# A Conformer block on one core: a ring of 12 query chunks, 15 probability tiles, the first input chunk in two DMAs, and a plan derived anew

## The chip, the cores and the metric

The kernel runs on one core of a Trainium2 chip. The core has five engines that work side by side and wait for each other through semaphores: TensorE (PE in the profile, with PEld for its weight loads), VectorE (DVE), ScalarE (ACT), GpSimd (POOL) and SyncE (SP, which here only issues DMAs). TensorE writes its results to PSUM, which this kernel uses as eight banks of 512 float32 columns; the other tensors live in SBUF, 128 partitions wide. The metric is the device time of one execution in microseconds (us). Lower is better.

## The reference

The input `x` has 2 sequences of 4000 tokens with 144 features, in bfloat16. The reference is one Conformer block:

```python
h = layernorm(x);  x = x + 0.5 * (silu(h @ w_ff1a) @ w_ff1b)         # 144 -> 576 -> 144
h = layernorm(x);  q, k, v = split(h @ w_qkv)                        # 4 heads of 36
p = softmax(q @ k.T * 36 ** -0.5);  x = x + (p @ v) @ w_o            # 4000 x 4000 per head and sequence
h = layernorm(x);  a, b = split(h @ w_pw1);  h = a * sigmoid(b)
c = sum over i of pad(h)[i : i + T] * dw[i]                          # 5 taps along the tokens
x = x + silu(c) @ w_pw2
h = layernorm(x);  x = x + 0.5 * (silu(h @ w_ff2a) @ w_ff2b)
return layernorm(x)
```

The attention is by far the largest part: 2 x 4 x 4000 x 4000 exponentials, 128 million of them.

## The kernel before

**Chunks.** The 8000 tokens are cut into 16 chunks of 500 (`NCH` = 16, `CH` = 500), eight for each sequence (`CPB` = 8). A chunk is stored as 4 blocks of 125 tokens. Everything except the attention works on one chunk at a time: `pre(c)` makes the first feed-forward and the projections to queries, keys and values; `post1(c)` takes the attention's result through `w_o` and the gated linear unit; `post2(c)` makes the convolution, the second feed-forward, the last layernorm and the store.

**Attention.** For a chunk of queries the kernel goes through the keys of its sequence in 62 tiles of 64 keys and a last one of 32. The scores of one tile for all four heads are four matmuls of 64x64 weights and 500 columns (`scores`, L1731), each in its own quarter of the PE array, into a pair of PSUM banks. The exponential of a tile is taken in one of two ways:

- On ACT (`emit_exp`, L1758): one ACTIVATE with Exp over 1000 columns, from the pair of banks into one slot of `PT`. There are 806 of these, and 16 of 500 columns for the last tiles.
- On DVE (`dve_tile`, L1772): two TENSOR_SCALAR of 500 columns that turn the scores into 16-bit integers whose bits are an approximate power of two, then two bit operations and one product over 1000 columns, with the result split over two slots of `PT`. There are 186 of these tiles.

The probabilities are then multiplied with the values (`o_quads`, L1808): four matmuls for each used slot of `PT` (eight for a DVE tile, as it leaves two slots), which add up over all tiles of the chunk in the last two PSUM banks (`BX` = 6). A column of ones in the values gives the sum of the softmax. So a DVE tile takes one exponential off ACT, and costs five DVE instructions and four matmuls more on PE.

**Buffers that the change touches.** `PT` has `NPT` = 11 slots (L592). `QT` (L754) holds the projected queries of all 16 chunks, 2 x 8000 columns of bfloat16. It also serves as scratch memory: when a chunk c is finished, `epilogue(c)` (L1668) copies the two PSUM banks as float32 over the queries of chunks c-1 and c (`OTF`, L1670), which are no longer needed, and transposes them from there. The first two chunks are processed in two halves (`phases`, L1718: first the keys of the first five chunks, then the others, since the later keys come late); the sums of the first half wait in `SAVE` (L1658), which lies over the queries of later chunks. `proj` (L1258) computes queries and keys; a condition keeps a projection from being issued while its place still holds `SAVE`.

**What sets the order.** At build time a planner runs through the whole kernel with its own costs for every operation. Each chunk's work is a generator that asks for an engine, a bank or a slot (`need`), and `pick_any` (L1912) chooses what comes next. Its choices are steered by `POLICY` (L603), 20 tables of 49 values, one for each stretch of 21 key tiles; `due` (L2005) decides by them whether a tile goes to DVE. The planner records the operations. After that, `reorder` (L283) moves blocks of operations on each engine by the offsets written in `ORDER` (L38), one character for a block, and `PLACES` (L115) assigns the PSUM banks. `R.cut()` begins a new block. In the end every engine has a fixed list of instructions; it runs this list in order and waits at an instruction whose inputs, slot or bank are not ready. All instructions are emitted by one helper, so the profile puts nearly all of them on L402 and they are told apart by tile names.

**Start and end.** At the start SP loads `X` chunk by chunk (L841 for chunk 0), while ACT issues the loads of the first weights. In the end, when no attention is left, the planner switches to a mode ("tail") in which SiLU is taken by ACT directly; for this a dummy activation on `DUM` (L2063) loads the other function table. Before that, SiLU is made of a Tanh on ACT (tile `TH`) and a product on DVE (tile `HT`, `SW`).

Of the kernel before, what the change touches and what calls it, by code (L numbers as in the profile page):

```python
# [21 lines left out]
TB = 125  # L22
# [12 lines left out]
FILLS = (5, 2, 5, 12, 3, 1, 3, 0, 0, 0, 0, 0, 0, 0)  # L35
# [16 lines left out]
        "MPPPPWOPPQOXJPPVOJOOYQNIOOOOPNPPPSOSOPQQUQOGPZPPPPQHPPaOJOOOXNQQMMVZMMMEMNUNPNLOPTOOROMSOZNTPLRRMMIO"
        "]OOOOQOMOOOOQYMOOOOQOMOQOPPPPPPSOOOPPTPNPNPPPPQQNPPPPPPPPYYVPRLJP]]HPITOPNQJMOSgOSSORKTLQNd2RKMMRLNS"
        "SLMQQRJSNRY]LOPPM:SOMKPQLPQQNRROMRRRMVLQNNXO_LNNNNNNPPRLNNZQQSPTINOHSPLRRMaTLPPLLRTTLLLMSLNVVOWOMORW"
        "ENSVVN[MJNRMOVVOMOMOSQORROR^RNRROR)JNRNNNRROQRRJNRRRNWSJNOMOQNYOOOPSMNXMMOSNNOMZSNNNPMOPWMNVNNNNNOdP"
        "NOOQQMQLNOOOOORPNLPPPPQOZOPPPSSPIVVQQNVOQUUOQN??RSOZOKOOOROOLQNPPPRO^QMNQQMWOKNOMNRRORVINQQMMQQNWTQM"
        "NLNSPSQKWQOURPW[QUQQTRX>DRR@QEQQQQQaPPPPPPPR=QRLLQOLXXNNNOOLNRRRRMYSOZNDOLOYNOXNNGNNNNOgQNROOPUOPNXQ"
        "QLBKNOMNPNSSOOLZRNNSPPMUUOGPWJPPJUOQQ^QKHOOPNRRMTROJJQOPPPZOOSNNNPZOOJOOOOOPNROOPPPPPQOPPPPQTQMNOPPP"
        "TOOOSNPVMUNNOMNRRNNQORR[NLOZNNNNNNRTLL_LP`LNPQLXPJORINIOQUHOQVMMPNOOPTOQNNPQRROUPTOOOQQQTTWPMMYOO:NO"
        "OOOQZPPPPPPZPNORTNP?USPIKNP_OOOOOOOOOSOPNKQOPPPQRP[LOOOOOPQOPKYOOOOQNNOZNQNNOOOPPRLOPPPPPQOPPQOPPPPP"  # L60
        "PPPPPPTOPNOWWOQWNOIWWOGRIOMVP[GQYNQWJRLFSSKRTIPEQTMPNORORNOPROQNQOQQVPUKNNNNXbNNNNNNNNOQNNOROOQQQQHP"
        "bOOQNNOOOOSZNNPJLRPMKQRMQSPLOPPRROTROJRROVJOOPSSNUU]OOSTTObEQQLFYQQM`LNNNNNYP/LNNNNNNPPROOSQXNLOOQNN"
        "OPROOPP]OOOQQNLSN]^LMKNNOMPMOQKRRXQUHPPIOK_OOOOOOOOOOOQNNPQYNOOQRM]RKRSQISQWJFOROIiMOPROOK^XXMMMMNNX"
        "MSPGMI^>MOPQQLQQNJPQRRKXPPTJNNNNPQQNPPPZOPNYPMMOMNNOOPPPPPQQRPSQOI]O[NNNYMOOQNNQHUZDOOOPPQQG_LPPMOOP"
        "NOQNNZNNOOOXNNNO[LNNNOOOOOOWNOWOMYMMMQMMVOMNOOOQTNOOOPROOPPVOOYNOOLOOOOQTXLNOQOPJOXOOOOQOMOWSPURKKLU"
        "LOXPNLOOOPQMQQNQRNOUQNPMQQQQKSQUSQSVMWPGETYOKSJPNSYRNFKQWMMOMQUMRLNRROTQINUUQNSJLMRRTMVRcMTHNRSNSFNO"
        "ZFOOLPMRVKSLLOWLPPMQUMVVKMMPLMWTQMMMUMQUUMNINRRLNPPPRRSZMOJPPMPeMNNUPMOOORROQSEZIPMXJMNNNSULQKLSNPNP"
        "ZOOSNNOMOPNPPPPPPPPPPPRRTQVKQNPRGSPPKSOORNOPPPPQOPPPPPPPQQQSSPRRRGWRSQTTTKBHYRJRNQKYOOJTNNNNRMQNQQTM"
        "OZNNYOMWMOOOJOIPTO[RNLMOWRNLROTWZOGGMNOWOKNPTTQNLWPVPDPNUNQHNO[QRSLLORKQNLPPSOOOUQRMOQQQQRPFPPPPROOP"
        "TQNPMQTPQORPQSQOEQORRTVPLQQHTKOOOPQOPROOPPPPPPVOPPMOOPQQNPUOQQMRRKNSXOOLQNPMOPPQOPQOWQNRMNSQRMJPTPNP"  # L70
        "NPPPPTTNOVVRRNJMTPTUVNORJNSSOO8YOOOOPRMNNPPUURNNKTQKUUQMJMUQQQRRHJPSSNNaM`NNPPLLPSYPJJVNNPPSSSSSSL??"
        "PPPPTTTOOSQIIggPNLNQQMSLNVMMQQRRR@TTGGDQMROOPPSOOOQSSPLMQQN"
    ),
    "act": (
        "PPPPPPPPPPPPPPSOOOSQNNPQOPPQOPQOPWOOOOOOOPPPQRRTLMSUSLLSLMOPPPPPPPPPPPPQOPPQOPPPPPPPPQOPPPPPPPPPPPPP"
        "PPPQOPPPPPPPPPPPPPPPPPPPPPPPPPPPPPPPPPPPPPPPPPPPPPPPPPPPPPPPPPPPPPPPPPROOROQNPQOPPPPPPPPPPPPPPPPPQOP"
        "QQNPPQOPPPPPPPPPPPPPPPPPPPPPPPPPPQOQOQOPPPPPPPPPPPPROOPPPPPPPPPPPPPPPPPPQOPPPPPPPPPPPPPPPPPPPQOPPPPP"
        "PQOQOPPPPPPPPQOPPPPPPPPPPPPPPPPPPPPPPQOPPPPPPPPPPPPPPPPPROQNPQQNPPPPPPPPPPPPPQOPPPPPPPPQOPPPPPPPPPPP"
        "PPPPPPPPPPPPPPPPPSOOOPPPPPPPPPPPPPPPPPPPPPPPPPPPPPPQQNPPPPQOPPPPQQNPPQOPPQOPQOQOPPPPQOQOPPPPPPPPPPPP"
        "PPPPPPPPPPQOPPPPPPPPPPPPPPPPPPPPPPPPPPQOPPROOPPPPPQOPPPPPPPPPPQOPPPPPPPPPPPPPPPPPPPPPPPPPPPPPQOPPPPP"  # L80
        "QOQOPPQOPPPQOPPPPPPPPPPPPPPPPPPPPPPPPPPPPPPPQQNPPPPPQOPPPPPPPPPPPPPPPPPPPPPPPPPPPPPPPPPPPPPPPPPPPPPP"
        "PPPPPPPPPPPPPPPPPPPPPQOPPPPPPPPPQOPPPPPPPPQOQOQOPPPPPPPPPPPPPPPPPPPPPPPQOPPPPPPPPPPPQQQMPPPPPPPPPPPQ"
        "OQOQOPPPPPPPPPPPPPPPPPPPPPPPQOPPPPPPPPPPPPPPPPPPPPPPPPPPPPPPPPQOPPPPPPPPPPQOPPPPPPPPPPPPPPPQOPPPQOPP"
        "PPPPPPPPPPPQOPPPPPPQOPPPPPPPPPPPPPPPPPPPPPPPPPPPPQOPQOPPPPPPQOPPPPPPPPPPPPPPPPPPPPPPPPPPPPPPPPPPPQOP"
        "PPPPPPPPPPPPPPPPPQOPPPPPPQOQOPPPPPPPQOPQOQTNPNOPROQNQQQMPPPPROOSQNNPQSNOSSSLMMPPPPPPPPPQQNPPROO"
    ),
    "dve": (
        "PQRPQQQJPROQaMOOOQRaMNJNOPLRNNYYHOOKNPIRNQJQQNRROQQQQIWSPPR_OaPGGOQQKQKTWSNSTEGWRSENFNVQRLMXMNORNNPM"
        "QQNPQOPQOPPPROOPPPPQOPPPPPPPPPQOQOPPRPRSQRRTQQRRSTPSSTRURUQRURRSTRSWSQRVSUVQSUU$US2T!DSQoTQOPSQOS@SC"
        "MRLRPQyRHNQGLOLNNOMNOPNOOOPNPNPQMPRORNOPrOOPQRLRLR=OLPNOPNOPNOOOOOOOWOMOMOPLQRRMSPLOPPSPPQQQVPPPPPDP"  # L90
        "PPQOPPQOROOQOQOROOQOPcPNOOOOPQOQKNOOOOPNQOQQTMVNNPMOOPPPPQQVPSPJRRKRSQSTPUUWNSF@LLOPPPPPUPUPPQRIQQRP"
        "QRWQNQOPP=QOPPPROOPUPNOPNPPPPQQ_PLOOQNPPLO]NOOLOOPNOOSQMQLSOROQRRRNRGVNQOQOKPPPPPPPPPPTOTOOLOPPRPQSS"
        "OSSPLRPDRPNPPPPPQOPQOQRROQQQQHROQQQQQVQOGOTOMPQQSQRNQQRROSSASNRXQRPRTOSSSS@RJRSOR=QRPRSOHSPRSQJQRPTP"
        "SOOXRBNNPNOSNOSNOSNPNPROOSOOOPQOQOTPNOOVOOQNPMPPPVPNPPMOPROOZQNPQOPQOPGPPPPQOPPPPPPQOPPPPQOPPPPPQQTP"
        "URUQTKPEQQGROOUQOQOQTPTOORDNQOQOPQQNRSOTLNOOSOOOQOQSPTQKPTPJROSPRRNQQTPTRNRSQSQTHP9O`PPQOPPPPPPEOOPN"
        "PRPNQOQOQOPPPPPPQOPPPPPPROOTOOOORRNSMPNPROOPPPPPRfNNOPNPNOOOOOOPQMNOOSNNOPPPPPPPPPQOROOPPPPRRNRPQKPP"
        "PPUOOOROMQRNORPNPQOQQNSOOOPQOQRNQRMQNQQNPPPPPROOPPPPPQOTPPPRKOPQOQOPPVPPVOOOPPSQENSOOOPPPPPSQORPRPRP"
        "RPUDOQORPQQTPPPQDPQOPPPROOPROOQQNQOPPQOPPPPPPQOPPPPPPPPPPPPPPPPQOPPTYPTLSPJKLOPPQOPPRORNOROOPPPPPPPP"
        "PPQQQQQKQRNOPPPQOPPQOPPTPPMOROOQOQOSOOSNOOPPPPPUOOOOOPVOPPPLpNOOOPWOLNNNNNNOPNOOOOQNQMQMQOLOQQRMRNOP"
        "PPPPPPPPPPPPPPQOQOROOROQNPPPPPQOPPROOPPPPPPPPPPPPQOPPPPQOPPPPPPPPPPPPPPROOPROQQMPPPPQQNRTNSMRMRLOPPQ"  # L100
        "OPQOXPRPRPJRRIQLPPPQOPQOPPQOPQOPSPNRPRPRPQHPSOORNOPQOQORPNUROMNQNUPNTNOPLRROMQOPSSNRMMPPQOPPPPPPSOOO"
        "PPPROOQOPPPPPPPXPQOPPSOOQFQOPPPPPPQOQOSOSOTQSMINPPPQRNOQOUOOORORLTNPSMPVPKPNPRMOQOPQOQQNRPRPLPPPRSNP"
        "RPKPQOQOPPQOPPROOSOOOPROOQOQQQQQRPTPPSOSOBOPPPROSNPSPPSTRSMRRKCRPQMPROQNPQOPPPPPRTOMPQRLOQOQQQSQSeMO"
        "PQOPScUNNOPSPGQQSST4EHSNROSPSEV[]OQ_RSFGOHSGINKQNQRSKPYPQJNOQNNO"
    ),
    "pool": (
        "PQQQQRSOPRPQTQOPQQSPROQQQQQRROQQQQQQQ,PXOOOOOOOXNOQNTM[NLMSNNOPLPNQTQMSMPWPQOPHWTMQLMPSPUOHQOQUKPPPQ"
        "QJPQQQMPPQOQOSOOSNOQNPPRPNQQN"
    ),
    "sp": (  # L110
# [448 lines left out]
def bass_standalone__conformer_family_zipformer__speech_kernel(  # L559
# [1108 lines left out]
    def epilogue(c, part):  # L1668
# [27 lines left out]
        for zz in range(2):  # L1696
            bk = yield need("pe", banks, dur=0.44)
            for i in range(NB):
                if i == 2:
                    R.cut()  # L1700
# [406 lines left out]
```

## Time and profile before

| what | us |
|---|---|
| median of 3 runs (883.4 to 884.31) | 883.54 |
| the profiled execution, its whole time | 883.61 |
| its span, first to last instruction | 881.5 |
| PE busy, instructions | 852.0, 11403 |
| ACT busy, instructions | 850.7, 1096 |
| DVE busy, instructions | 815.1, 1799 |
| POOL busy, instructions | 300.0, 584 |

The share that a busy time has of the span is an average over three parts: the first 20 us, in which the attention has not started; the attention until about 846 us; and 35 us behind it, in which the last chunks are finished. Two instructions that follow each other on ACT or DVE overlap in the records: the next one starts before the one in front has ended. So the duration that a group row gives (1084 ns for the large exponential) is longer than the time by which the engine's queue moves on, which is read from starts in the timeline. The granted clock of TensorE is 0.998 of the full one.

### The profile page before, as it was taken

The page shows a single profiled execution, that of the slowest core. Times are in us where ns is not written, and L with a number is a line of the kernel's source. Part 1 is how long each engine was busy: PE and PEld are TensorE (multiplying, and loading weights), DVE is VectorE, ACT ScalarE, POOL GpSimd, SP SyncE. Part 2 cuts the span into 40 slices and gives each one's busy share as a digit, 9 for nine tenths or more (in the row PEclk, how much of TensorE's full clock was granted, in tenths as well). Part 3 has the DMA queues.
Part 4 walks back from the last instruction along what each step waited for, and adds up shares of the span by engine and source line. Part 5 has one row for each costly group of instructions (what it writes and reads, how often), then busy time and mean ns, then how long its engine had stood idle before and what let it go on. Part 6 is the DMA issues. An engine that isn't in the chain of part 4 may idle for free.

```text
span 881.5 us, 26988 instructions
## 1 busy us (share of the span) xinstructions
PE 852.0 (97%) x11403; PEld 378.4 (43%) x11403; DVE 815.1 (92%) x1799; ACT 850.7 (97%) x1096; POOL 300.0 (34%) x584
## 2 busy tenths in 40 slices
PE   8999999999999999999999999999999999999996
PEld 6544333444344434334344344443433343444465
DVE  7978999999999999989988899997988999999997
ACT  6799999999999999999999999999999999999984
POOL 7761600215235324125203432045351036031434
PEclk9999999999999999999999999999999999999999
DMA  3231010201211210211101111002011001101101
GB/s 100 44 66 36 22 37 2 63 22 39 51 30 23 51 24 14 52 24 39 28 17 30 30 29 31 23 16 51 22 37 23 15 9 37 24 22 37 30 23 33
DMA packets 114221, 28.80 MB, mean 33 GB/s; under 512 B 101085, under 2 KB 114100, under 8 KB 114100
## 3 DMA queue, kind: packets, MB, share of 16 engines
q1 hardware_dynamic: 112642, 26.46, 13.7%
q8 instruction: 89, 1.46, 0.7%
q10 hardware_dynamic: 1458, 0.62, 0.3%
q14 instruction: 32, 0.26, 0.1%
HBM read 13.44 MB, written 13.61 MB: 31 GB/s over the span
## 4 chain that ended last, share of the span: by engine, by line
ACT 45%; PE 33%; DVE 19%; DMA 1%; issue 1%; SPq 1%; ACTq 0%; DVEq 0%
ACT PT L402 40%; PE PS L402 33%; DVE PT L402 11%; ACT TH L402 4%; DVE HT L402 2%; DVE ST L402 1%; DVE X L402 1%; DVE XN L402 1%; DVE QT L402 1%; SPq L402 1%; DVE KT L402 1%; DMA X<-in_x_dram 1%; DVE AN L402 0%; DMA XTQ<-rows 0%; DMA WE<-in_w_ff1a_dram 0%
## 5 line engine op out<-in xcount | busy, mean ns | idle before, releaser
L402 ACT ACTIVATE PT<-PS 128x1000 bf16<-128x1000 f32 (+1 forms) x822 | 758.2, 1075 | 1.7 <-PE PS L402 0.6
L402 PE MATMUL PS<-QT,KT 64*64 64x500 bf16 x3968 | 424.6, 385 | 13.1 <-ACT PT L402 7.5
L402 PE MATMUL PS<-PT,VA 64*37 64x500 bf16 x4712 | 411.6, 372 | 2.5 <-DVE QT L402 0.7
L402 DVE TENSOR_SCALAR PT<-PS 128x500 int16<-128x500 f32 x372 | 243.9, 668 | 8.7 <-PE PS L402 6.9
L402 PEld LDWEIGHTS PS<-QT,KT 64*64 64x64 bf16 x3968 | 124.8, 104 | 238.1 <-ACT PT L402 137.1
L402 POOL TENSOR_SCALAR RS<-ST 125x4 f32<-125x4 f32 x130 | 35.2, 271 | 466.0 <-DVE ST L402 459.7
L402 PEld LDWEIGHTS PS<-PT,VA 64*37 64x37 bf16 x4712 | 140.0, 96 | 100.7 <-DVE PT L402 23.1
L402 DVE TENSOR_SCALAR PT<-PT 128x1000 uint16<-128x1000 uint16 x372 | 150.7, 415 | 1.9 <-PE PS L402 0.7
L402 POOL TENSOR_SCALAR XN<-X,RS 125x144 bf16<-125x144 bf16 x260 | 148.2, 602 | 6.8
L402 DVE TENSOR_TENSOR PT<-PT 128x1000 bf16<-128x1000 bf16 x186 | 125.9, 678 | 1.3
L402 ACT ACTIVATE TH<-PS 128x500 bf16<-128x500 f32 (+3 forms) x198 | 107.0, 562 | 7.0 <-PE PS L402 5.8
L402 POOL TENSOR_TENSOR RS<-RS,NHALF 125x4 f32<-125x4 f32 (+1 forms) x93 | 93.0, 1004 | 32.9 <-DVE RS L402 27.2
L402 DVE SCALAR_TENSOR_TENSOR HT<-TH,PS 128x500 bf16<-128x500 bf16 (+1 forms) x135 | 80.8, 615 | 16.8 <-ACT TH L402 15.9
L402 PE MATMUL PS<-XT,WA 128*128 128x500 bf16 (+5 forms) x288 | 74.8, 365 | 0.6 <-ACT PT L402 0.2
L402 DVE BATCH_NORM_STATS2 ST<-X 125x6 f32<-125x288 bf16 x160 | 65.5, 446 | 3.0 <-DMA X<-in_x_dram 2.9
L402 DVE SCALAR_TENSOR_TENSOR X<-PS,X 125x288 bf16<-125x288 f32 (+1 forms) x128 | 56.6, 449 | 8.4 <-PE PS L402 7.8
L402 PE MATMUL PS<-WB,HT 128*125 128x144 bf16 (+1 forms) x640 | 52.0, 230 | 0.2 <-ACT HT L402 0.2
L402 PEld LDWEIGHTS PS<-WB,HT 128*125 128x125 bf16 (+1 forms) x640 | 44.3, 136 | 12.9 <-issue 3.7
L402 PEld LDWEIGHTS PS<-XT,WA 128*128 128x128 bf16 (+1 forms) x288 | 20.8, 97 | 33.4 <-issue 13.3
L402 POOL COPY U<-U 128x2 bf16<-128x2 bf16 (+1 forms) x54 | 11.1, 241 | 68.0 <-DVE U L402 68.0
L402 DVE STREAM_TRANSPOSE XN<-XN 128x320 f32<-128x320 f32 x54 | 27.0, 499 | 2.2 <-POOL XN L402 2.2
L402 PE MATMUL PS<-U,DG 128*128 128x375 bf16 (+6 forms) x204 | 28.1, 263 | 0.1
(93 smaller groups left out, 521.4 us busy)
## 6 DMA issues: line engine op xcount, KB each, us to landing
rows<-XN SPq DMA_DIRECT2D x216, 40.0 KB, 2.0
XT<-rows SPq DMA_DIRECT2D x56, 128.0 KB, 2.0
rows<-AN SPq DMA_DIRECT2D x60, 40.0 KB, 2.0
X<-in_x_dram SPq DMA_DIRECT2D x16, 140.6 KB
XTQ<-rows SPq DMA_DIRECT2D x26, 70.3 KB
out_dram<-XN SPq DMA_DIRECT2D x13, 140.6 KB
XT<-rows SPq DMA_DIRECT2D x56, 16.0 KB, 1.9
out_dram<-XN SPq DMA_DIRECT2D x3, 70.3 KB
```

The source lines that it names most:

```text
L402: ins = getattr(eng, o.name)(*o.a, **o.k)
```

## The change

The change has four parts.

1. `QT` becomes a ring of `NQR` = 12 chunks: chunk c uses place c modulo 12, so chunks 12 to 15 use the places of chunks 0 to 3. `SAVE` and the scratch place of chunk 0 move to the places of chunks 8 to 11, and the conditions in `proj` follow: the queries of chunks 8 to 11 wait until chunk 0 has been transposed (`turned`), those of chunk c from 12 on until chunk c-11 has.
2. The memory goes to `PT`, which gets 15 slots.
3. `X` of the first chunk is loaded by two DMAs of two blocks each, with a semaphore for each.
4. All tables are new: `POLICY` (all 20 except a few values), `ORDER`, `PLACES`. Blocks in the middle of a group of matmuls are no longer cut (`R.cut()` is gone from `residual`, `mm2`, `ff_tile`, `proj` and `epilogue`), the planner no longer charges SP for late loads, and the ACT instructions that use SiLU in the tail are tied behind the dummy activation (`gated`), which is tied behind the last 40 exponentials.

What the changed program holds, counted from its instruction lists: 802 large exponentials on ACT (806 before), 190 tiles on DVE (186), 4728 matmuls on the values (4712), and in the tail 2 convolutions more with SiLU on ACT and 6 more normalisations on ACT (`XN<-X`) instead of DVE. All other counts are the same, apart from the split DMA.

```diff
-    NPT = 11
+    NPT = 15
+    NQR = 12
...
     POLICY = {
         "DGAP": (
-            2.0, 2.0, 2.0, 4.0, 2.5, 2.5, 2.5, 2.5, 2.5, 3.25, 3.25, 3.25, 3.25, 3.25, 3.25, 2.5,
+            3.0, 3.0, 3.0, 3.0, 2.5, 2.0, 2.5, 1.5, 2.5, 2.5, 3.25, 3.25, 3.25, 3.75, 1.5, 1.5,
...
-    QT = sb("QT", [2, N])
+    QT = sb("QT", [2, NQR * CH])
...
-    load_x("sp", 0)
+    op("sp", "dma_start", X[0:TB, 0:2, :], x_tok[0][:, 0:2, :], q="x0", w=[("X", 0, 0), ("X", 0, 1)], cost=0.45, lat=2.9)
+    op("sp", "dma_start", X[0:TB, 2:NB, :], x_tok[0][:, 2:NB, :], q="x0b", w=[("X", 0, 2), ("X", 0, 3)], cost=0.0, lat=2.9)
...
-    R.free["sp"] += 0.45 * len(later)
...
+    gate, exps = [None], []
+
+    def gated(o):
+        if gate[0] is not None:
+            o.deps.append((gate[0], False))
...
-            R.cut()
             for t, (l, rh) in enumerate(terms[i]):
...
-        over = nm == "WQ" and p == 1 and c >= CPB
-        late = nm == "WQ" and p == 0 and c >= NCH - 4
-        bk = yield need("pe", banks, dur=0.42, cond=(lambda: not saved) if over or late else None)
+        over = nm == "WQ" and CPB <= c < NQR
+        late = nm == "WQ" and c >= NQR
+        bk = yield need("pe", banks, dur=0.42, cond=(lambda: 0 in turned) if over else (lambda: c - NQR + 1 in turned) if late else None)
...
-        qd = QT[:, :, c * CH:(c + 1) * CH]
+        qd = QT[:, :, c % NQR * CH:(c % NQR + 1) * CH]
...
-    SAVE = QT[:, 1, T:T + 4 * CH * NQ].bitcast(F32).rearrange("p (c k n) -> p c k n", c=NQ, k=2)
+    turned = set()
+    assert NQR * CH - T == 4 * CH and NQ == 2
+    SAVE = QT[:, :, T:NQR * CH].bitcast(F32).rearrange("p c (k n) -> p c k n", k=2)
...
-        if c:
-            OTF = QT[:, :, (c - 1) * CH:(c + 1) * CH].bitcast(F32)
-        else:
-            OTF = QT[:, 0, N - 4 * CH:N].bitcast(F32).rearrange("p (z n) -> p z n", z=2)
+        q0 = (c - 1 - (c % NQR == 0)) % NQR
+        OTF = QT[:, :, q0 * CH:(q0 + 2) * CH].bitcast(F32) if c else SAVE[:, 0, :, :]
...
+        turned.add(c)
...
-    op("act", "activation", DUM[:, :], NHALF[:, 0:1], ACT.Silu, bias=0.0, scale=1.0, r=["NHALF"], w=["DUM"], cost=1.5)
+    gate[0] = op("act", "activation", DUM[:, :], NHALF[:, 0:1], ACT.Silu, bias=0.0, scale=1.0, r=["NHALF"], w=["DUM"], cost=1.5)
+    gate[0].deps += [(o, False) for o in exps[-40:]]
```

More of the change, by code (lines that the diff above doesn't have):

```diff
@@ L1558, in conv_act @@
             yield need("act")
-            op("act", "activation", dst, PSV[0:rows, bk, 0:n], ACT.Silu, bias=0.0, scale=1.0,
-               r=[("ps", bk)], w=[(key, z)] + list(wk), cost=c_act(n))
+            gated(op("act", "activation", dst, PSV[0:rows, bk, 0:n], ACT.Silu, bias=0.0, scale=1.0,
+               r=[("ps", bk)], w=[(key, z)] + list(wk), cost=c_act(n)))
             banks.give(bk)
@@ L1733, in scores @@
         b = c // CPB
-        k0, q0 = t * KT_ROWS, c * CH
+        k0, q0 = t * KT_ROWS, c % NQR * CH
         kcs = {min(k0 // CH, CPB - 1), min((k0 + KT_ROWS - 1) // CH, CPB - 1)}
```

200 lines of the change are left out of this document (96 added, 104 removed), and 126 rows, old and new, of the table POLICY.

## The prediction

> **What bounds the kernel now.** I read the engine totals first, then a table of stretches, then the groups of ACT in the long middle, then starts in the timeline, and last who waited for whom. The totals do not decide: PE and ACT both read 97%.
>
> ```profile
> PE 852.0 (97%) x11403; PEld 378.4 (43%) x11403; DVE 815.1 (92%) x1799; ACT 850.7 (97%) x1096; POOL 300.0 (34%) x584
> ```
>
> Busy time by stretch (us; instructions in brackets):
>
> ```profile
> 0.00:100.00 100.00, 94.59 (x1205) 48.86 (x1209) 81.57 (x211) 86.97 (x130) 62.40 (x135) 1.00 0.25 58
> 100.00:200.00 100.00, 96.76 (x1338) 39.02 (x1334) 98.29 (x215) 99.67 (x120) 12.20 (x22) 1.00 0.13 30
> 200.00:440.00 240.00, 237.60 (x3248) 99.22 (x3236) 232.46 (x491) 238.94 (x293) 84.49 (x158) 1.00 0.16 34
> 440.00:720.00 280.00, 273.19 (x3652) 115.86 (x3648) 251.66 (x521) 279.30 (x352) 84.31 (x169) 1.00 0.12 26
> 720.00:846.00 126.00, 122.30 (x1666) 51.88 (x1658) 121.01 (x256) 125.21 (x154) 44.31 (x82) 1.00 0.13 29
> 846.00:881.50 35.50, 27.58 (x323) 23.55 (x322) 30.11 (x109) 20.61 (x53) 12.31 (x20) 0.96 0.12 30
> ```
>
> The columns are PE, PEld, DVE, ACT, POOL. From 100 to 846 us ACT is never seen idle. Busy records overlap, though, so its true slack has to be worked out. From the timeline I take how far ACT's queue moves on per instruction:
>
> ```profile
> 309.20 0.27 ACT L402 ACTIVATE TH<-PS 64x125 bf16<-64x125 f32 x1
> 309.50 8.18 ACT L402 ACTIVATE PT<-PS 128x1000 bf16<-128x1000 f32 x9
> 317.47 0.69 ACT L402 ACTIVATE TH<-PS 128x500 bf16<-128x500 f32 x1
> 317.94 1.12 ACT L402 ACTIVATE PT<-PS 128x1000 bf16<-128x1000 f32 x1
> ```
>
> Nine exponentials take 317.47 - 309.50 = 7.97 us, 0.886 each; a Tanh of 500 columns 0.47; one of 64x125 0.30. The groups between 100 and 840 us:
>
> ```profile
> L402 ACT ACTIVATE PT<-PS 128x1000 bf16<-128x1000 f32 x741 | 690.1, 1086 | 1.3 <-PE PS L402 0.3
> L402 ACT ACTIVATE TH<-PS 128x500 bf16<-128x500 f32 x105 | 66.7, 657 | 0.9 <-PE PS L402 0.3
> L402 ACT ACTIVATE PT<-PS 128x500 bf16<-128x500 f32 x15 | 9.8, 652 | 0.2 <-PE PS L402 0.2
> ```
>
> 741 x 0.886 + 120 x 0.47 = 713 us; the rest (19, 15 and 13 small Tanh at 0.26, 0.30 and 0.16) adds 11.5: 724 of 740 us. ACT is full but for 16 us, 2%. PE, whose 97% includes the overlapping tails of its matmuls, mostly waits for banks that ACT frees:
>
> ```profile
> PEld PS L402 <- ACT PT L402: 149.7, 411, 1.0
> PEld PS L402 <- DVE PT L402: 69.6, 220, 0.8
> ```
>
> So ACT sets the pace, DVE comes close between 100 and 200 us (98%), and the last 35 us are a chain of their own. The sum below is made against the profiled execution (883.61), which stands 0.07 above the median.
>
> **The change, part by part.** Both programs have fixed lists, so instructions can be counted between the same marks: up to the last exponential that chunk 2 needs (early), from there to the last exponential of all (late), and behind it (tail). In the profile the marks fall near 195 and 846 us.
>
> *ACT, late.* 4 large exponentials fewer (649 to 645): 4 x 0.886 = 3.5. 5 Tanh of 500 columns fewer (94 to 89; 3 are moved to the early part, 2 become SiLU in the tail): 2.3. One of 64x125 fewer: 0.3. Together -6.2 us on the engine without slack.
>
> *ACT, early.* 3 Tanh of 500 and one of 64x125 more: 1.4 + 0.3 = +1.7. The exponentials are equal (160).
>
> *DVE.* A tile costs, from starts in the timeline (302.37 to 303.56 for two TENSOR_SCALAR, 305.07 to 305.40 for a bit operation, 301.40 to 302.00 for the product), 2 x 0.595 + 2 x 0.33 + 0.60 = 2.45 us. Late it gets 4 tiles (+9.8), and 4.2 us of other work leaves for the early part: +5.6. Between 200 and 846 us DVE is idle for 7.5 + 28.3 + 5.0 = 41 us, so I cost this at nothing; chunk by chunk its work in the new list (40.6 to 48.2 us) stays under ACT's in every late chunk, where the old list had one chunk over it (53.2 against 48.7). If that cover is gone, it costs its +5.6 in full; if the levelling helps, the sum over the chunks of the larger of the two falls from 638 to 628, -10.6 in place of -6.2. Early, DVE gets +3.2 (4 statistics, 2 transposes, 2 residuals, 2 gates more, one TENSOR_SCALAR fewer), in a stretch where it is 98% busy. By ACT the early part costs +1.7, by DVE +3.2, and by the larger of the two in each phase of the first chunks +0.1. I take ACT's +1.7, the middle.
>
> *PE.* 16 matmuls on the values more, in four rounds of four. Matmuls of 500 columns start 0.21 us apart where the array is full, so +0.8; but rounds in which only half of the array is used get fewer, 2225 rounds in all become 2219. It changes between attention and other work oftener: 774 runs become 798. What matters is whether the scores come late for ACT: I summed, from the spacing of the matmul records, PE's work between the scores of neighbouring exponentials. It exceeds ACT's by over 0.17 us in 52 places before (14.6 us together) and in 55 after (17.2). In the trace such places cost ACT about a quarter of their excess, the rest is absorbed by the exponential in flight. So +0.7; bounds 0 and +3.
>
> *15 slots.* Matching waits with the list, the last thing that came for 781 of the 795 exponentials between 60 and 840 us was their own scores, for 14 a slot; those 14 lost 0.3 us. More slots are worth 0 to -0.3 by themselves: 0.
>
> *The ring.* Queries of chunks 12 to 15 now wait until chunks 1 to 4 have been transposed, which in the trace is over by 300 us, and these queries are first read behind 600 us. DVE's in-order queue holds the projection's copy at its place in the list, behind work that comes first anyway: 0. `SAVE` moves without a change of instructions: 0.
>
> *X in two DMAs.* DVE's first statistics wait for it:
>
> ```profile
> 4.62 0.46 DVE L402 BATCH_NORM_STATS2 ST<-X 125x6 f32<-125x288 bf16 x1 [2.38 <-DMA X<-in_x_dram]
> 5.19 0.45 DVE L402 BATCH_NORM_STATS2 ST<-X 125x6 f32<-125x288 bf16 x1
> ```
>
> The list of DMA issues gives size and median time to landing (us) of two loads:
>
> ```profile
> XT<-rows SPq DMA_DIRECT2D x56, 128.0 KB, 2.0
> XT<-rows SPq DMA_DIRECT2D x56, 16.0 KB, 1.9
> ```
>
> A transfer of 16 KB lands no sooner than one of 128 KB, so half the bytes gain little: -0.2. If the 3.9 us from issue (0.74) to 4.62 were all bytes, it would be -1.9; if the second half comes after 5.19 by the length of its issue, +0.5. SP's later loads stand behind one more issue (0.45 us), but the next two wait for the weights until 5.18 anyway.
>
> *Tail.* The work is nearly the same: 319 matmuls against 316. DVE, the busiest with 30.1 of 35.5, loses 6 normalisations and 2 products, and gains a few small ones: -1.2 at its spacings. ACT gains 2.8 but has 15 us free. The old tail ends on 8 normalisations in a row on DVE (875.02 to 876.99); half of them go to ACT, beside it. -0.5; bounds -1.2 and +2.8.
>
> Sum: -6.2 + 1.7 + 0.7 - 0.2 - 0.5 = -4.5 of 883.6: **879.2 us**, 0.5% faster.
>
> **The rivals.**
>
> *More slots close the bubbles of ACT.* By the rows above a slot was hardly ever what an exponential waited for, so this can only act through the planner, which may issue scores sooner if results may lie longer. All 16 us gone would give 879.2 - 16 = 863; half of them, 871. Against it: PE's over-long gaps did not get fewer. "Consistent bubbles", says the Trainium skill (Perfetto Trace Analysis, Optimization Strategy), on the engine that should be saturated can mean that there aren't enough buffers. By that rule the four slots would give those 863 us; the trace does not bear it out, as it puts 0.3 us on slots.
>
> *Nothing is left.* The early part pays DVE's +3.2, and the excess on PE comes through in full (+3) while the tail gains nothing: -6.2 + 3.2 + 3 = 0, 883.6.
>
> *DVE becomes the bound late.* In 200 to 440 us DVE is busy 97%, in 720 to 846 96%; these are 57% of the late time. If DVE decides there, ACT's gain counts for 43% (-2.7) and DVE's +5.6 for 57% (+3.2), and early DVE's +3.2 holds: 0.5 + 3.2 + 0.7 - 0.7 = +3.7, 887.3. It turns the sign once DVE decides in some 40% of the late time. For it: banks that DVE empties held PE up for 69.6 us already. Against it: the new list spreads the tiles more evenly (chunks 8 and 11, which had 10 and 9 of them, now have 12 and 13).
>
> **How the numbers follow.** The forecast, 876.5 to 881.8, gets 0.47; the bubbles 0.12, all of it faster; nothing left, 881.8 to 885.3, 0.14; DVE as the bound, or as late an order, 0.27. What a measurement can tell from no change is about 0.2%, 1.8 us. Faster: 0.47 + 0.12 = 0.59; same 0.14; slower 0.27. The range goes from half of the bubbles closed (870) to just over the DVE case (888), which leaves about a tenth on each side.
>
> **What would show it.** In the profile after, ACT should have 802 large exponentials and the same idle share in the middle, so that the last exponential starts near 840.7 instead of 844.7 us; the first one near 19.6 instead of 19.8; the stretch behind the last one as long as before. If exponentials start more than 0.886 apart on the mean by more than now, with waits on `PT` that DVE frees above 69.6 us, the third rival holds. If ACT's slack between 100 and 840 us falls well under 16 us, the first does. What would make the sum wrong is a new order whose waits I can only bound: a tenth more or less in ACT's slack is 1.6 us.

## The result and the profile after

The changed kernel takes 881.7 us (median of 22 runs, 880.49 to 885.28), the kernel before 883.98 (22 runs, 883.4 to 885.0). The ratio is 0.9977, with a 95% interval of 0.9971 to 0.9983: 0.23% faster, about 2.0 us, where 4.5 had been forecast. The profiled execution took 882.33 us, its span is 880.5.

The engine totals of the changed kernel, from its page:

```profile
PE 851.5 (97%) x11419; PEld 380.2 (43%) x11419; DVE 822.7 (93%) x1812; ACT 849.6 (96%) x1098; POOL 300.4 (34%) x584
```

Its busy time by stretch, in the same columns as before (PE, PEld, DVE, ACT, POOL):

```profile
0.00:100.00 100.00, 91.78 (x1157) 49.32 (x1157) 81.20 (x206) 84.23 (x127) 53.74 (x116) 1.00 0.23 53
100.00:200.00 100.00, 97.93 (x1317) 38.95 (x1316) 98.33 (x219) 98.58 (x119) 30.60 (x53) 1.00 0.18 40
200.00:440.00 240.00, 237.70 (x3272) 99.45 (x3274) 230.01 (x485) 238.79 (x292) 74.06 (x146) 1.00 0.16 32
440.00:720.00 280.00, 274.41 (x3682) 118.83 (x3672) 264.41 (x553) 278.81 (x351) 93.91 (x178) 1.00 0.12 27
720.00:845.50 125.50, 121.29 (x1671) 49.77 (x1670) 119.02 (x250) 125.35 (x154) 36.11 (x76) 1.00 0.11 24
845.50:880.50 35.00, 28.35 (x332) 23.85 (x330) 29.77 (x105) 23.86 (x60) 12.02 (x18) 0.96 0.12 31
```

Part of the loss shows in the first line: ACT is busy for 84.23 us of the first 100, where it was 86.97 before. The groups of ACT between 100 and 840 us, and PE's waits for banks over the whole span (us, times, longest):

```profile
L398 ACT ACTIVATE PT<-PS 128x1000 bf16<-128x1000 f32 x740 | 690.9, 1085 | 3.0 <-PE PS L398 1.5
L398 ACT ACTIVATE TH<-PS 128x500 bf16<-128x500 f32 x104 | 68.4, 673 | 0.0
```

```profile
PEld PS L398 <- ACT PT L398: 148.3, 406, 1.1
...
PEld PS L398 <- DVE PT L398: 68.9, 223, 0.8
```

One exponential and one Tanh fewer than before stand in these 740 us: by the same spacings as in the prediction, ACT's slack there is about 17 us, where it was 16. So with the additional slots no bubbles were closed. DVE holds PE up for 68.9 us, where it was 69.6, and between 200 and 845 us for 55.2, where it was 60.5: DVE did not become the bound late.

The span can be cut at five marks that both programs have: the first exponential; the 97th ACT instruction of the plan, up to which both plans hold the same ACT instructions; the start of the last exponential that chunk 2 needs; the start of the last exponential of all; the end.

| stretch | before, us | after, us | difference |
|---|---|---|---|
| head, to the first exponential | 19.80 | 19.29 | -0.5 |
| front, to the end of the 97th ACT instruction | 53.9 | 57.4 | +3.5 |
| middle, to chunk 2's last exponential | 119.7 | 123.6 | +3.9 |
| late, to the last exponential | 651.3 | 644.0 | -7.4 |
| tail | 36.7 | 36.2 | -0.5 |

Head, late part and tail gained 8.4 us, and the two stretches between gave most of it back. These are two executions; the profiles of the runs below, cut at the same marks, agree on most of it. Wherever a run leaves the stretch as it is, the middle takes 119.7 to 119.8 us with the old plan (three profiles) and 123.4 to 123.6 with the new one (nine). The late stretch takes 651.3 to 651.6 with the old plan and 644.0 to 645.8 with the new one (eleven), and the tail 36.7 to 36.8 and 36.2 to 36.5. Busy time in these stretches, first of the kernel before:

```profile
19.80:73.70 53.90, 52.22 (x622) 24.16 (x622) 43.91 (x104) 49.08 (x74) 33.65 (x65) 1.00 0.26 56
73.70:193.40 119.70, 116.22 (x1632) 46.94 (x1634) 115.73 (x252) 119.31 (x143) 24.42 (x45) 1.00 0.12 27
193.40:844.73 651.33, 638.29 (x8625) 269.71 (x8618) 611.38 (x1280) 648.96 (x802) 215.47 (x413) 1.00 0.14 30
```

and of the changed kernel:

```profile
19.29:76.70 57.41, 52.41 (x622) 24.65 (x620) 45.60 (x106) 49.81 (x75) 35.17 (x68) 1.00 0.25 54
76.70:200.30 123.60, 120.92 (x1654) 49.25 (x1654) 121.04 (x264) 122.08 (x147) 36.22 (x63) 1.00 0.15 33
200.30:844.28 643.98, 631.88 (x8610) 267.42 (x8609) 613.02 (x1284) 641.44 (x792) 202.92 (x392) 1.00 0.13 29
```

The front holds the same work and takes 3.5 us longer: there something waits. In the middle all three engines are busy for longer: PE +4.7 us, DVE +5.3, ACT +2.8. In a stretch that is 3.9 us longer and almost full, busy time would grow by itself; but the counts are higher too, by 22 matmuls, 12 instructions on DVE and 4 on ACT. The late part has less on PE (-6.4) and ACT (-7.5).

**Where the front waits.** POOL's queue, before and then after (start, duration, releaser of the idle time in front):

```profile
13.11 2.18 POOL L402 TENSOR_TENSOR RS<-RS,NHALF 125x2 f32<-125x2 f32 x3 [0.19 <-DVE RS L402]
...
16.23 1.01 POOL L402 TENSOR_TENSOR RS<-RS,NHALF 125x4 f32<-125x4 f32 x1
```

```profile
12.27 4.40 POOL L398 TENSOR_TENSOR RS<-RS,NHALF 125x2 f32<-125x2 f32 x6 [4.36 <-DVE RS L398]
...
17.60 1.01 POOL L398 TENSOR_TENSOR RS<-RS,NHALF 125x4 f32<-125x4 f32 x1
```

The first layernorm that goes through POOL as a whole (125x4) is behind six small powers in place of five (two more of them stand ahead of the three shown), and the last of its statistics ends on DVE at 16.68 us instead of 15.23; it is 1.4 us late. Its result goes to memory and back by DMA (`rows<-XN`, `XT<-rows`). SP's issues, before and after:

```profile
20.67 2.67 SPq L402 DMA_DIRECT2D rows<-XN  x4
25.81 0.83 SPq L402 DMA_DIRECT2D XT<-rows  x2
```

```profile
22.41 3.25 SPq L398 DMA_DIRECT2D rows<-XN  x4
27.07 0.83 SPq L398 DMA_DIRECT2D XT<-rows  x2
```

The same happens again before 75 us: the issue of `XT<-rows` at 63.62 us before is at 65.99 after. PE's list has the matmuls that read it ahead of scores, and PE stands still:

```profile
69.73 1.08 PE L398 MATMUL PS<-XT,WA 128*128 128x500 bf16 x4 [0.94 <-DMA XT<-rows]
...
72.88 0.59 PE L398 MATMUL PS<-XTQ,WK 72*128 72x500 bf16 x2 [0.90 <-DMA XTQ<-rows]
```

Then ACT stands still as well, for 0.69 and 0.61 us:

```profile
70.39 1.07 ACT L398 ACTIVATE TH<-PS 128x500 bf16<-128x500 f32 x2 [0.69 <-PE PS L398]
...
73.86 4.59 ACT L398 ACTIVATE PT<-PS 128x1000 bf16<-128x1000 f32 x5 [0.61 <-PE PS L398]
```

The first of these two waits of PE is the new order's: all fifteen profiles of this document that have the new front show it, with 0.6 to 1.3 us, and none of the four with the old front. The second is in three of the fifteen only, and those three end the front latest. ACT also idles for 3.34 us in front of 32.19 us, where the kernel before has 2.37 us in front of 32.43.

### The profile page after: what moved, and what is told of

Its sections match the earlier page's. It is cut to its first block, busy times and chain, and to the rows that moved or that the text cites. A ratio compares the mean times of both kernels' runs of the same rounds, so it can differ in the third digit from the quotient of the medians.

```text
span 880.5 us, 27000 instructions
## 1 busy us (share of the span) xinstructions
PE 851.5 (97%) x11419; PEld 380.2 (43%) x11419; DVE 822.7 (93%) x1812; ACT 849.6 (96%) x1098; POOL 300.4 (34%) x584
## 4 chain that ended last, share of the span: by engine, by line
ACT 46%; PE 33%; DVE 17%; POOL 2%; DMA 1%; issue 1%; SPq 1%; POOLq 0%; DVEq 0%
ACT PT L398 42%; PE PS L398 33%; DVE PT L398 7%; ACT TH L398 4%; DVE HT L398 2%; DVE ST L398 2%; DVE X L398 2%; DVE XN L398 2%; POOL RS L398 1%; POOL XN L398 1%; DVE KT L398 1%; DVE QT L398 1%; DVE AN L398 1%; SPq L398 1%; DMA rows<-XN 0%
## 5 line engine op out<-in xcount | busy, mean ns | idle before, releaser
L398 DVE TENSOR_SCALAR PT<-PS 128x500 int16<-128x500 f32 x380 | 250.1, 668 | 5.8 <-PE PS L398 3.9
L398 PEld LDWEIGHTS PS<-QT,KT 64*64 64x64 bf16 x3968 | 123.4, 104 | 236.8 <-ACT PT L398 137.1
L398 POOL TENSOR_SCALAR RS<-ST 125x4 f32<-125x4 f32 x130 | 37.0, 284 | 482.2 <-DVE ST L398 475.6
L398 DVE TENSOR_SCALAR PT<-PT 128x1000 uint16<-128x1000 uint16 x380 | 154.5, 418 | 2.1 <-PE PS L398 0.8
L398 POOL TENSOR_SCALAR XN<-X,RS 125x144 bf16<-125x144 bf16 x260 | 150.4, 610 | 13.1 <-DMA out_dram<-XN 6.4
L398 DVE TENSOR_TENSOR PT<-PT 128x1000 bf16<-128x1000 bf16 x190 | 128.8, 679 | 1.3
L398 PE MATMUL PS<-XT,WA 80*128 80x500 bf16 (+5 forms) x288 | 74.5, 365 | 2.2 <-DMA XT<-rows 0.9
L398 PE MATMUL PS<-U,DG 128*128 128x250 bf16 (+6 forms) x204 | 29.6, 264 | 0.0
L398 POOL COPY U<-U 128x2 bf16<-128x2 bf16 (+1 forms) x54 | 9.2, 209 | 46.3 <-DVE U L398 46.3
```

The source lines that it names most:

```text
L398: ins = getattr(eng, o.name)(*o.a, **o.k)
```

## Experiments

Each run is compared with runs of the kernel before on the same chip. "Against the changed kernel" is the difference of its ratio to 0.9977, times 883.8 us; the two intervals leave 1.0 to 1.3 us on each such difference. Where a stretch of the profile is compared instead, it lies between the marks of the table above.

### X in two DMAs, alone and undone

```diff
-    load_x("sp", 0)
+    op("sp", "dma_start", X[0:TB, 0:2, :], x_tok[0][:, 0:2, :], q="x0", ...)
+    op("sp", "dma_start", X[0:TB, 2:NB, :], x_tok[0][:, 2:NB, :], q="x0b", ...)
```

In the kernel before:

> The kernel before with one part of the change alone: X of the first chunk in two DMAs; the plan and the order of every engine stay those of before. Theory as forecast: the first BATCH_NORM_STATS2 starts near 3.9 us instead of 4.62, the second near 4.9 instead of 5.19, the first exponential 0.2 to 0.5 us earlier than 19.80, and of that nothing to 0.5 us reaches the end: 883.4 to 884.0. Rival: the ninth issue on SP's queue makes the other X late and the front loses, 884.2 to 884.6.

Measured: 884.33 us against 883.77, ratio 1.0007 (0.9999 to 1.0016). That lies in the rival's range, but the rival's reason is not in the profile: the statistics of the next chunk start at 8.65 and 9.87 us, where they started at 9.10 and 10.05, so that `X` is not late. The first exponential comes at 21.21 us all the same, behind a stretch of lowered clock (last section). Of the eleven executions, the three with a mean granted clock of 0.995 or 0.996 took 884.99 to 885.74 us, the others, with 0.997 or 0.998, took 883.21 to 885.05.

In the changed kernel, the other way:

> The changed kernel with that part undone: X of the first chunk in one DMA again. If the two DMAs are worth what the head of the trace shows (first exponential 19.29 against 19.80), it comes out 0 to 0.6 us behind the changed kernel: 881.7 to 882.3. If the split is what cost the front its time, it comes out ahead of it: 878.5 to 880.5.

Measured: 881.9 us, ratio 0.998 (0.9971 to 0.9988), 0.3 behind the changed kernel. The statistics do start earlier with two DMAs. These are the changed kernel's; with one DMA they start at 4.59 and 5.49 us in it, and at 4.62 and 5.19 in the kernel before:

```profile
3.91 0.46 DVE L398 BATCH_NORM_STATS2 ST<-X 125x6 f32<-125x288 bf16 x1 [2.09 <-DMA X<-in_x_dram]
...
4.90 0.46 DVE L398 BATCH_NORM_STATS2 ST<-X 125x6 f32<-125x288 bf16 x1
```

But the first exponential starts at 19.08 us in the changed kernel with one DMA, and at 19.29 with two. So the head's 0.5 us is not the doing of part 3 of the change, and by these two runs part 3 is worth nothing that can be measured.

### The front's order, put back and transplanted

Up to 76 us of the plan both programs hold the same 1220 operations (the split DMA apart). So the order and the banks of this front can be exchanged, with nothing else changed. The blocks are cut again as before (`R.cut()`), and the tables begin like those of the kernel before; 66 of the first 124 digits of `PLACES` differ.

```diff
     "dve": (
-        "PPROQQQLPPPUUNNNNSMUNNPNOQOSPNSUMOPLOPTPNPNPPQQQQQQQQHPVPRPLPLPPPRSSNRNQVPUOODNUMPNPNPPQSPMXNOOQNNOO"
+        "PQRPQQQJPROQaMOOOQRaMNJNOPLRNNYYHOOKNPIRNQJQQNRROQQQQIWSPPR_OaPGGOQQKQKTWSNSTEGWRSENFNVQRLMXMNORNNPM"
...
 PLACES = (
-    "4540352315301235404310523035204320244354321123203214052534114030254011540241204124012410314032034023"
+    "5304235415231501253015424035304230043214020532141052312043340552105410450241204124012401314032034023"
```

> The changed kernel, with the order of the blocks and the banks of the first 76 us of the plan put back to those of the kernel before; there the two plans hold the same instructions, so nothing but the order differs. Behind it everything is the changed kernel's. Theory A, the front's new order loses time that nothing gives back: the 97th ScalarE instruction ends near 73.5 us instead of 76.66, and the end moves by the same 3 us, to 878.2 to 879.3. Rival B, the end is set by what comes later (TensorE busy 97% of the span) and a delay in the front is absorbed: 881.2 to 882.2.

Measured: 880.12 us against 883.77, ratio 0.9956 (0.9943 to 0.997): 1.9 us ahead of the changed kernel. (Its profiled execution was disturbed and took 884.96; the last section shows how.) The same with one DMA:

> The changed kernel with the front's order of the kernel before (as in the run that gave 880.12) and X of the first chunk in one DMA as well, so that up to 76 us it is the kernel before. If the split brings what its undoing cost the changed kernel (0.2 us), 880.1 to 880.6; if the split only pays together with the front order derived for it, equal or better: 879.4 to 880.1.

Measured: 880.86 us against 883.97, ratio 0.9966 (0.9954 to 0.9978). That is outside both ranges, and 1.2 us ahead of the changed kernel with one DMA (0.998), its like in all but the front's order. Two DMAs are 0.9 us ahead of one here, no more than the intervals allow. The profile with one DMA, the front and all that follows up to the last exponential:

```profile
19.93:73.75 53.82, 51.91 (x620) 23.61 (x620) 44.79 (x106) 49.06 (x74) 33.81 (x65) 1.00 0.26 57
73.75:845.20 771.45, 754.95 (x10280) 317.42 (x10279) 735.16 (x1550) 765.93 (x941) 242.31 (x463) 1.00 0.14 29
```

53.82 us, as in the kernel before (53.90). Now the reverse, the kernel before with the new front's order:

> The kernel before with the changed kernel's order and banks in the first 76 us of the plan, and nothing else changed (X in one DMA): the transplant the other way round. If the front's new order is what costs the changed kernel 1.6 us, it costs here as much: 885.0 to 886.0. If the gain of the transplant came from the seam with the later plan instead, 883.6 to 884.3.

Measured: 885.78 us against 883.97, ratio 1.002 (1.0011 to 1.0028): 1.8 us lost. In its profile the first exponential starts at 19.28 us, with one DMA: the head's gain belongs to the order. Every chunk's last exponential comes 2.3 to 2.7 us later than in the profile of before, so the loss of the front is carried to the end, neither absorbed nor increased.

Theory A holds in both directions: the new order of the front costs 1.2 to 1.9 us in the three pairs. It forecast 3, so that 880.12 lies between its range and the rival's; the profiled execution of the changed kernel happened to lose more there than the others. In the fifteen profiles that have the new front order, the 97th ACT instruction ends between 75.0 and 76.9 us, at 75.8 on the mean (76.66 in the changed kernel's own); with the old order it ends at 73.69 and 73.75 (left out are two more profiles with the old order, whose clock was lowered). That is 2.0 us on the mean, head and front together.

### One engine relieved, early and late

Each run takes work from one engine of the changed kernel: eight exponentials over half their columns (ACT 8 x 0.417 = 3.3 us less, by starts in this run); scores and products with V of 14 or 16 tiles over half their columns (PE, 0.21 us a tile); eight DVE tiles over half their columns (1.10 us a tile by starts, 8.8 in all). The cuts below are for the early stretch. The first is from the run with all three engines; the run with ACT alone picks the same eight exponentials by their count.

```diff
+        if n in (73, 84, 96, 108, 120, 132, 145, 158):
+            src, dst = PSV[:, lo, 0:CH], PT[:, pt, 0, :]
...
+        w = CH // 2 if n in (73, 79, 84, 90, ...) else CH
-            op("pe", "matmul", PSV[64 * p:64 * p + 64, bk, 0:CH], ...
+            op("pe", "matmul", PSV[64 * p:64 * p + 64, bk, 0:w], ...
...
+        z, w = None, CH // 2 if n in (86, 102, 110, 126, 133, 144, 152, 165) else CH
```

> The changed kernel with eight exponentials between 100 and 180 us (the 65th, 75th, ... 135th) over 500 columns instead of 1000; half of their probabilities keep the values of an earlier tile, so the output is not the reference's. Each takes 0.43 us off ScalarE (0.886 less 0.46), 3.4 in all. If ScalarE is what this stretch waits for, as the sum of the forecast had it, nearly all of it reaches the end: 878.2 to 879.2. If TensorE or VectorE sets the pace there, less than half does: 880.2 to 881.7.

> The changed kernel with the scores and the products with V of 16 tiles between 100 and 180 us over 250 columns instead of 500; the output is not the reference's. 3.3 us less for TensorE there. If TensorE paces this stretch (the eight short exponentials there brought only 0.7 of 3.4 us): 878.4 to 879.8. If it is neither ScalarE nor TensorE but VectorE, on whose results TensorE's queue waits: 880.8 to 881.7.

(Two of the 16 tiles are last tiles, which the edit does not reach: 14 tiles, 2.9 us.)

> The changed kernel with eight of VectorE's tiles between 110 and 185 us computed over half their columns (2.4 us of work each down to about 1.3, some 9 us in all); the output is not the reference's. If VectorE, 97 to 99% busy there, paces the stretch: 876 to 879. If ScalarE and TensorE pace it: 880.8 to 881.7.

> The changed kernel with eight late exponentials (every 40th from the 401st, 435 to 715 us) over 500 columns instead of 1000; half of their probabilities keep an earlier tile's values, so the output is not the reference's. 3.4 us less for ScalarE. If ScalarE alone paces the late part, as the term late -6.2 of the forecast has it: 878.3 to 879.0. If TensorE's queue paces it there, as the early run of this kind showed for 100 to 180 us: 880.8 to 881.7.

> The changed kernel with the scores and the products with V of 16 late tiles (every 20th exponential from the 401st) over 250 columns instead of 500, exponentials untouched; the output is not the reference's. 16 x 2 rounds x 0.104 us = 3.3 us less for TensorE. If TensorE paces the late part: 878.4 to 879.5. If ScalarE paces it: 881.2 to 881.9.

### Several engines relieved together

> Both of the foregoing at once: 3.4 us less for ScalarE and 3.3 us less for TensorE in the late part; the output is not the reference's. If either engine alone paces it, the result is that of its own run. If the two are in balance, so that each takes over as soon as the other is relieved, each run alone moves little and this one moves most of 3.3 us: 878.4 to 879.5.

> The changed kernel with the same eight late exponentials over 500 columns (3.4 us of ScalarE), and the scores and V products over 250 columns for the tile of each and for the next one (16 tiles, 3.3 us of TensorE), so that both engines are relieved by the same 0.42 us in the same place; the output is not the reference's. Where the two were relieved in places 20 tiles apart, 1.5 of 3.3 us came. If a tile takes the larger of what the two need, place by place: 878.3 to 879.2. If VectorE is a third in the balance: 879.8 to 880.6.

> The changed kernel with all three engines relieved in the same eight late places: the exponential halved (3.4 us of ScalarE), scores and V products of it and the next tile halved (3.3 us of TensorE), and the nearest tile of VectorE halved (some 9 us); the output is not the reference's. ScalarE and TensorE together brought 1.35 of 3.3 us. If VectorE is the third in the balance, the rest comes now: 878.3 to 879.3. If what is left is the order itself (waits for results of other engines that no engine's work sets): 879.9 to 880.6.

> The same for the stretch from 100 to 180 us: 3.4 us less for ScalarE, 3.3 us less for TensorE, some 9 us less for VectorE, each in the same eight places; the output is not the reference's. Alone they brought 0.7, 0.5 and 0.7 us. If the stretch is paced by all three in turn, so that work moved into it costs what the slowest of them needs: 878.3 to 879.5. If their gains only add up: 879.6 to 880.2.

### Work added to one engine

These runs add work whose results nobody needs, in the same early stretch; the lists of all engines are otherwise the same.

```diff
+        if n in (73, 84, 96, 108, 120, 132, 145, 158):
+            op("act", "activation", JUNK[:, :], PSV[:, lo, 0:CH], ACT.Exp, ...)
...
+            scores(n, 0, lo, 0.0)
+            scores(n, 1, hi, 0.0)
...
+            if hh and n in (86, 102, 115, 129, 144, 157):
+                op("dve", "tensor_scalar", JUNK[:, :], PSV[:, bk, 0:CH], EXP_BIAS, 0.0, ...)
```

> The changed kernel with eight more exponentials over 500 columns between 100 and 180 us, into a buffer that nobody reads: 3.7 us more for ScalarE and nothing for the others. If a stretch costs what the slowest of three balanced engines needs, work added to one of them costs nearly all of itself: 884.4 to 885.6. If there is room on ScalarE, as much as taking 3.4 us off it brought (0.7): 881.9 to 882.6.

> The changed kernel with the scores of 14 tiles between 100 and 180 us computed twice into the same banks: 14 rounds of 0.21 us, 2.9 us more for TensorE and nothing for the others. Balanced engines: 883.7 to 884.8. Room on TensorE: 881.7 to 882.5.

> The changed kernel with six more 500-column reads of PSUM by VectorE between 100 and 185 us, into a buffer that nobody reads: 3.5 us more for VectorE and nothing for the others. Balanced engines: 884.2 to 885.3. Room on VectorE: 881.7 to 882.5.

### What the twelve runs gave

| run | work taken or added, us | median, us | ratio to before (95%) | against the changed kernel, us |
|---|---|---|---|---|
| early, ACT less | -3.3 | 881.04 | 0.9968 (0.9956 to 0.9981) | -0.8 |
| early, PE less | -2.9 | 881.24 | 0.9973 (0.9964 to 0.9982) | -0.4 |
| early, DVE less | -8.8 | 880.96 | 0.9967 (0.9955 to 0.9979) | -0.9 |
| early, all three less | -3.3 / -3.3 / -8.8 | 878.27 | 0.9937 (0.9925 to 0.995) | -3.5 |
| late, ACT less | -3.3 | 881.8 | 0.9976 (0.9966 to 0.9985) | -0.1 |
| late, PE less | -3.3 | 881.11 | 0.9969 (0.9958 to 0.998) | -0.7 |
| late, ACT and PE less, partly in other places | -3.3 / -3.3 | 880.16 | 0.9958 (0.9945 to 0.997) | -1.7 |
| late, ACT and PE less, in the same places | -3.3 / -3.3 | 880.35 | 0.996 (0.9948 to 0.9971) | -1.5 |
| late, all three less | -3.3 / -3.3 / -8.8 | 879.83 | 0.9955 (0.9942 to 0.9969) | -1.9 |
| early, ACT more | +3.7 | 884.75 | 1.0009 (1.0 to 1.0018) | +2.8 |
| early, PE more | +2.9 | 883.89 | 1.0002 (0.9993 to 1.001) | +2.2 |
| early, DVE more | +3.5 | 885.04 | 1.0014 (1.0006 to 1.0023) | +3.3 |

Set against the expectations: each of the three early runs with less work on one engine fell into the range that puts the pace on the other engines, and the three with added work into the range for balanced engines. The early run with all three (878.27) just reached the range for a pace set by all three (from 878.3). Late, ACT less and PE less lie 0.1 us outside the range for a pace set by another engine. ACT and PE together missed the range for a balance of two; in the same places they fell into the range with DVE as a third.

The profiles of the early runs, cut at the marks, say much the same with less noise. The middle takes 123.4 to 123.6 us in the nine profiles that leave it as it is:

| run | middle, us | against 123.5 |
|---|---|---|
| ACT less | 123.1 | -0.4 |
| PE less | 123.3 | -0.2 |
| DVE less | 122.4 | -1.1 |
| all three less | 120.8 | -2.7 |
| ACT more | 126.3 | +2.8 |
| PE more | 124.6 | +1.1 |
| DVE more | 126.5 | +3.0 |

**Early, a balance of the three is shown, with some room on PE.** Less work on one engine brings an eighth of itself or less in the middle (a quarter at most by the medians); on all three together it brings 2.7 of the 3.3 us (3.5 by the medians). More work costs 2.8 of 3.7 us on ACT and 3.0 of 3.5 on DVE, but only 1.1 of 2.9 on PE. In that profile PE also waits 1.37 us for the DMA `XT<-rows` in front of 246.97 us, some 65 us behind the added work, where the changed kernel has no such wait; from there on it is about 1 us later still. The work added to ACT and DVE also reads a PSUM bank once more before PE gets it back (5.2 us of PE's waits are for the added exponentials), so its price is that of the engine's time and of the bank's together; no run parts the two. ACT's queue shows how a relief is lost. Waits between 100 and 181 us in the changed kernel, and with the eight short exponentials:

```profile
PEld PS L398 <- ACT PT L398: 16.9, 46, 0.8
...
ACT PT L398 <- PE PS L398: 0.9, 3, 0.6
```

```profile
PEld PS L398 <- ACT PT L398: 12.2, 32, 0.8
...
ACT PT L398 <- PE PS L398: 2.3, 7, 0.6
```

PE waits 4.7 us less for banks that ACT empties, and ACT now waits for scores 7 times instead of 3. With DVE's six additional reads it is the additional instruction for which PE waits, and ACT behind it:

```profile
PEld PS L398 <- DVE JUNK L398: 3.5, 5, 0.9
...
ACT PT L398 <- PE PS L398: 2.2, 6, 0.6
```

**Late, it is shown only in part.** By the medians ACT alone brings 0.1 of 3.3 us, ACT and PE together 1.5 to 1.7, and DVE adds no more than the intervals allow. The profiles agree in size: the late stretch takes 643.5 us with less on ACT, 643.9 with less on PE, 643.0 and 643.2 with less on both and 642.8 with less on all three, against 644.0 to 645.8 where it is left as it is. The relief in the same places brought no more than the relief in different ones, against the expectation, and the run with all three fell between its two ranges. What holds the rest there, waits of the fixed lists or DVE work farther from the chosen places, is not settled.

## Why the prediction was wrong, step by step

**ACT, early, +1.7: the step that failed.** The forecast priced the early part by the work that ACT gets more. With the -0.2 for `X` in two DMAs that made +1.5 for head, front and middle together. They measured +6.9 in the profiled pair, and about +5.9 with the mean of the fifteen profiles (2.0 up to the 97th ACT instruction, 3.9 behind it). Two things are in it.

- *The front's order, 1.2 to 1.9 us by the three pairs.* There the change moves no work at all, so a sum over instruction counts must give nothing. The forecast named the waits of a new order as what it could only bound, and gave them no term in the early sum. PE's wait for `XT<-rows` (0.6 to 1.3 us in every profile with the new front) is part of it.
- *Work moved ahead of 200 us, about 3.9.* The forecast charged it by ACT (+1.7), as the middle between "the larger of the two" (+0.1) and DVE's +3.2. It never counted PE there. Between the first exponential and the mark the new instruction list has 686 matmuls that don't belong to attention, the old one 660. The runs with added work show that ACT, DVE and, in part, PE each charge for what they get, and in the middle PE and DVE got more than ACT (busy for 4.7, 5.3 and 2.8 us longer). So the forecast's own +3.2 for DVE, which it set aside, was the nearest of its three prices. That the moved work is the cause is argued from these counts and prices, as no run moved it back; how the 3.9 us divide between DVE and PE stays open.

**ACT, late, -6.2, and PE, +0.7.** Together -5.5, measured -7.4. The size is near, the reason is only half right: "the engine without slack" is not what pays in full, as 3.3 us off ACT alone gave 0.1 by the medians and about 0.6 by the late stretch. What the trace shows beside it is that PE's busy time fell as well, by 6.4 us, beside ACT's 7.5: matmuls moved to the early part are missing here. That this is the cause was not tried by a run. The +0.7 for gaps between scores cannot be told apart from it. It was luck that the late part gave 1.9 us more than its two terms: with the forecast's -5.5 there, the early part as measured and the tail's -0.5, the change would have gained next to nothing.

**DVE, late, 0.** DVE's busy time there rose by 1.6 us and PE's waits for it did not (55.2 us between 200 and 845 us, where it was 60.5). No run speaks against it.

**X in two DMAs, -0.2.** Nothing that can be told from zero: -0.9, -0.3 and +0.6 in three pairs. The bound above zero was needed; the first statistics gain 0.7 us, and the chain behind them does not pass it on.

**Tail, -0.5.** It came as forecast: 36.7 to 36.2 us in the profiled pair.

**15 slots, 0, and the ring, 0.** No wait in the trace contradicts it. More slots alone weren't tried: their memory comes from the ring.

**The rivals.** The bubbles were not closed (about 17 us of slack against 16). The Trainium skill (Perfetto Trace Analysis, Optimization Strategy) reads consistent bubbles as possibly too few buffers; four slots more, with a new plan, left them as they were. DVE as the late bound is not seen. (In its sum, with +3.2 early, DVE would have to decide in 25% of the late time for the sign to turn; the 40% go with +1.7.) "Nothing is left" was nearest: its time began at 881.8, and its mechanism, the early part paying more than ACT's share, is half of what happened.

The same page of the Trainium skill (Perfetto Trace Analysis, Identifying the Most-Contended Engine) advises to optimize the engine with the highest occupancy first, and leaves PE's busy share out of this, judging PE by its weight loads (43% busy here). By that rule ACT, 96% busy, would be the one; the runs disagree: 3.3 us off ACT alone gave 0.1 late and 0.8 early.

**A version that beats both.** The changed kernel with the old front order is at 880.12 us, 0.44% under the kernel before (0.30 to 0.57%). The prediction had no such version, and it shows that the new plan behind 76 us was worth about twice what the whole change brought.

## What to carry to other kernels

Where three engines are each busy for about 98% of a stretch, the price of moved work is not its time on the busiest one. Here work added to a single engine cost between four and nine tenths of itself in the stretch, whichever engine it was, and removed work paid in the main only where all three were relieved. So count every engine's work in every stretch, gains and losses apart. Where two programs hold the same work up to a mark, compare the times at which they pass it; what differs there is order alone, and it can be put back by itself.

## What was not expected

**A gap of 1.8 us on PE, a halved clock, and 5 us.** In the profiled execution of the changed kernel with the old front order, PE waited 1.77 us for DVE:

```profile
14.13 0.41 PE L402 MATMUL PS<-IDENT,XN 125*72 125x125 bf16 x4 [1.77 <-DVE XN L402]
```

and the granted clock (the column behind POOL) was 0.50 from 16 to 28 us:

```profile
12.00:16.00 4.00, 1.94 (x22) 1.42 (x20) 3.93 (x18) 1.03 (x4) 3.35 (x6) 0.87 0.51 144
16.00:20.00 4.00, 4.00 (x26) 2.91 (x24) 2.90 (x10) 2.10 (x6) 3.67 (x8) 0.50 0.38 91
20.00:24.00 4.00, 4.00 (x42) 2.24 (x40) 1.21 (x3) 2.26 (x6) 0.54 (x2) 0.50 0.04 7
24.00:28.00 4.00, 3.52 (x26) 0.93 (x22) 2.75 (x9) 3.61 (x5) 3.30 (x7) 0.50 0.20 36
28.00:32.00 4.00, 3.94 (x35) 1.41 (x34) 3.37 (x10) 3.94 (x6) 3.77 (x8) 0.92 0.20 48
```

The first exponential started at 24.09 us (19.93 in the same kernel with one DMA), and the execution took 884.96 us against a median of 880.12. In the kernel before with two DMAs a gap of 0.99 us at the same place went with a clock of 0.62 between 16 and 20 us. In the changed kernel's profile the gap is 0.40 us and the clock stays at 1.00.

The length of a gap alone does not decide it. In the changed kernel with the old front and one DMA a gap of 1.10 us (shown below) leaves the clock at 1.00:

```profile
390.00:395.00 5.00, 3.90 (x62) 1.43 (x58) 4.34 (x10) 4.01 (x6) 4.61 (x8) 1.00 0.30 64
```

There PE is busy for 3.90 of 5 us around the gap. Between 12 and 16 us it was busy for 1.94 of 4 us where the clock was then halved, for 2.72 where it went to 0.62, and for 3.24 in the changed kernel, where it stayed. So it may be the low activity of PE over some us that brings the clock down; no run tried it.

**A DMA that lands 2 us late is paid by PE.** In the changed kernel with the old front and one DMA, the reload of a layernorm's result was issued 3.39 us after the last issue of its store (386.44). SP waited for that store to land, and PE for the reload:

```profile
383.89 2.55 SPq L402 DMA_DIRECT2D rows<-XN  x4
389.83 0.81 SPq L402 DMA_DIRECT2D XT<-rows  x2
```

```profile
392.76 0.63 PE L402 MATMUL PS<-XT,WP 128*128 128x500 bf16 x2 [1.10 <-DMA XT<-rows]
```

In the changed kernel the same step, from the last issue of the store to the issue of the reload, took 1.43 us:

```profile
386.95 2.55 SPq L398 DMA_DIRECT2D rows<-XN  x4
390.93 1.30 SPq L398 DMA_DIRECT2D XT<-rows  x2
```

The lead of the first profile over the changed kernel's, 2.9 to 3.1 us from 90 to 390 us, fell to 1.9 at this place (and to 1.3 near 530 us, where PE waited 0.6 us for another `XT<-rows`). So in a fixed list each execution keeps what chance takes from it, and a profile of one execution can be a microsecond off in the front alone.
